# Slots 8 to 31 as pairs of 64-row matmuls that trade banks midway, in an attention and bilinear feed-forward kernel on one core

## The chip, the core and the metric

One of the eight cores of a Trainium2 chip runs the kernel. TensorE (PE) multiplies, with a weight load (PEld) ahead of each matmul; ScalarE (ACT) does exp and copies, VectorE (DVE) multiplies and copies, GpSimd (POOL) and SyncE (SP) issue DMAs. The metric is the device time of one execution in microseconds (us); less is better. PSUM, into which TensorE writes, has eight banks of 512 fp32 columns in 128 partitions; SBUF holds everything else.

## The reference

```python
# q, k, v: (8, 8, 576, 64); bias_table: (32, 8); all fp32
scores = (1 / sqrt(64)) * q @ k.T                  # 576 x 576 for each batch and head
scores = scores + bias_table[bucket(|i - j|)]      # 32 buckets, the last from distance 128 on
attn = exp(scores - max); attn = attn / attn.sum(-1)
x = (attn @ v) as (8 * 576, 8 * 64)                # 4608 tokens, 512 wide
out = ((x @ w_a) * (x @ w_b)) @ w_out              # 512 -> 1536 -> 512
```

## The kernel before

**Attention.** A *slot* s handles one pair p of heads of one batch; there are 32 (eight batches of four). The two heads lie in SBUF partitions 0 to 63 and 64 to 127, so their score matmuls (64 rows of contraction each) are a *pair of 64-row matmuls*: one on the lower, one on the upper half of the array, into different PSUM banks. 576 positions are 512 "main" ones (four tiles of 128) and 64 "tail" ones. All exponentials are taken without a maximum; the bias enters as a factor exp(bias), multiplied on by DVE. The values carry a column of ones, so that the sum of the weights comes out as column 65 (`J = Dh + 1 = 65`).

**Feed-forward.** Tokens are handled in nine chunks of 512 (chunk c is batch c's main positions, the last one all the tails). A chunk has 12 blocks `df`: `pa` and `pb` (each four full matmuls, 128 rows, 512 columns, over `xn_sb`), then ACT copies pa (`ha`), DVE multiplies pb by it (`g_sb[df]`); then four outputs `po` of 12 matmuls each, which ACT copies to SBUF and stores by DMA. That is 144 full matmuls a chunk.

**Order.** It is written by hand: one string of tokens per slot, `steady[s % 4]`, and every engine executes its own instructions in that order. A prime (') means the pair of the slot before. In slots 8 to 31:

- Q0 to Q3 (`qk`, L412): the main scores of one key tile for both heads, into one score tile of two banks; E (`ex`, L440) its exp on ACT, M (`mul`, L446) the factor on DVE.
- R (`qk_rows`, L423): main keys by tail queries, four pairs; ER, MR exp and factor. K (`qk_tail`, L488): tail keys by all queries, 128-row matmuls, where `ZB` has zeros beside each head; EK, MK exp and factor.
- TL' (`av_tails`, L589): tail weights by values, five pairs of 64 rows by 65 columns into two banks, one for each head. A' (`av_head`, L599): main weights by values, 20 matmuls of 128 rows by 65 columns for head 0, then 20 for head 1; a number behind A or F says how many stand there. N0', N1' (`norm_head`, L611): reciprocal and scaling to `XG`, head by head, and then `t_x` (L638), which transposes XG into `xn_sb` by two DMAs on SP.
- F: the next matmul of the feed-forward's stream (`ff_part`, L936), H (`ff_ha`), G (`ff_g`), O and D (`ff_ob`, `ff_store`). F are strewn between the A's.
- MR', V and the loads: V copies values into place; q, k and v of later batches come by DMA from POOL and are transposed by DMA on SP (`t_half`, L388) into `QB`, `KB` and `ZB`.

Slots 0 to 7 and the first chunk stand in another string, `opening`; behind slot 31 the last pair's products (`av`, `av_mm`, its transposes on TensorE) stand between the remaining feed-forward units (`put_units`).

**PSUM.** Pool `ps_sc` has two score tiles of two banks, `ps_ff` two banks for the feed-forward, `ps_av` and `ps_tr` one bank each: the two of `two_banks`, used in turn by R, by TL and A, and by transposes.

Of the kernel before, what the change touches and what calls it, by code (L numbers as in the profile page):

```python
# [13 lines left out]
def kernel(  # L14
# [19 lines left out]
    NM = 4  # L34
# [374 lines left out]
    def shared(p):  # L409
        return p >= 8  # L410

    def qk(p, t0, ts=None):  # L412
        qT, kT, _ = operands(p)
        st[p].setdefault("at", [None] * NM)
        for t in ts or (t0, t0 + 1):
            ps = ps_sc.tile([128, 2, 512], FP32, tag="sc", name=f"qk{p}_{t}")
            for hh in range(2):
                r = slice(64 * hh, 64 * hh + 64)
                nc.tensor.matmul(out=ps[:, hh, :], lhsT=kT[r, t, :], rhs=qT[r, :, :],  # L419
                                 start=True, stop=True)  # L420
            st[p]["ps", t] = ps
# [66 lines left out]
    def qk_tail(p):  # L488
        qT, kT, z = operands(p)
        ps = ps_sc.tile([128, 2, 512], FP32, tag="sc", name=f"qkt{p}")  # L490
        if shared(p):
            nc.tensor.matmul(out=ps[:, 0, :], lhsT=z[:, 1, :], rhs=qT[:, :, :], start=True, stop=True)  # L492
            nc.tensor.matmul(out=ps[:, 1, 0:2 * ST], lhsT=z[:, 1, :], rhs=z[:, 0, :],
                             start=True, stop=True)
            st[p]["ps"] = (ps, None)
            return
# [15 lines left out]
    def ex_tail(p):  # L512
# [5 lines left out]
        if shared(p):  # L518
            nc.scalar.activation(out=at[:, 512:m + 2 * ST],
                                 in_=ps[:, :, :].rearrange("p a x -> p (a x)")[:, 0:SM + 2 * ST],  # L520
                                 func=ACTF.Exp, scale=scale)
            return
# [7 lines left out]
    def mul_tail(p):  # L530
        if not shared(p):
            mul_rows(p)
        at, wt = st[p]["att"], Wt_sb[:, p % 4, :]
        o = 512 + main_tail(p) - 128
        nc.vector.tensor_tensor(out=at[:, o:o + 256], in0=at[:, o:o + 256], in1=wt[:, 255::-1], op=MULT)
# [51 lines left out]
    J = Dh + 1  # L587

    def av_tails(p):  # L589
        b, hp = divmod(p, 4)  # L590
        st[p]["av2"] = banks = two_banks(f"av{p}")
        for jq in range(5):
            for hh in range(2):
                r = slice(64 * hh, 64 * hh + 64)
                nc.tensor.matmul(out=banks[hh][:, J * jq:J * jq + J], lhsT=weights_tail(p, jq)[r, :],  # L595
                                 rhs=vt[b % 2][r, hh, hp, :], start=(jq == 0), stop=True,
                                 skip_group_check=True)

    def av_head(p, hh):  # L599
        b, hp = divmod(p, 4)  # L600
        bank, v = st[p]["av2"][hh], vm[b % 2]

        def mm(jq, t):
            w = weights_last(p, t) if jq == 4 else weights(p, t, hh, jq)
            return lambda: nc.tensor.matmul(out=bank[:, J * jq:J * jq + J], lhsT=w,  # L605
                                            rhs=v[:, 2 * hp + hh, t, :], start=False, stop=True,
                                            skip_group_check=True)

        return [mm(jq, t) for jq in range(5) for t in range(NM)]

# [162 lines left out]
    def v_next(s):  # L773
# [135 lines left out]
    for token in opening.split():  # L909
# [26 lines left out]
    def ff_part(n):  # L936
        c, u, m = 1 + (n // 4 - 48) // 36, (n // 4 - 48) % 36, n % 4
        if u < 24:
            df, (w, kind) = u // 2, ((wa_sb, "pa"), (wb_sb, "pb"))[u % 2]
            if m == 0:  # L940
                ff[kind, df, 0] = ff_bank(f"{kind}{c}_{df}")
            nc.tensor.matmul(out=ff[kind, df, 0][:, :], lhsT=w[df // 4][:, m, 128 * (df % 4):128 * (df % 4) + 128],  # L942
                             rhs=xn_sb[m][:, 512 * c:512 * c + 512], start=(m == 0), stop=(m == NMC - 1))
        else:
            tt, part = divmod(u - 24, 3)
            if part == 0 and m == 0:
                ff["po", tt] = ff_bank(f"po{c}_{tt}")
            df = 4 * part + m
            nc.tensor.matmul(out=ff["po", tt][:, :], lhsT=g_sb[df][:, 128 * tt:128 * tt + 128],  # L949
                             rhs=wo_sb[:, df, :], start=(df == 0), stop=(df == NDF - 1))  # L950
        if m == 3 and (u < 24 or u % 3 == 2):
            ff["done"][u] = c

    ff["done"] = {}
    ff["mm"] = 4 * nxt
    ff["skip"] = 108 - sum(int(x[1:]) for k in (1, 2, 3) for x in steady[k].split() if x[0] == "F")

    def slot_step(s, token):
        name, num = token.rstrip("'0123456789"), "".join(x for x in token if x.isdigit())
        if name in ("F", "A"):  # L960
            for _ in range(int(num)):
                if name == "F" and ff["skip"] > 0:
                    ff["skip"] -= 1
                elif name == "F":
                    ff_part(ff["mm"])
                    ff["mm"] += 1
                elif av_queue:
# [54 lines left out]
    load_slot = {bb: 9 if bb == 3 else 12 if bb == 4 else 4 * bb - 5 for bb in range(3, B)}  # L1022
    while ff["skip"] < 0:
        ff_part(ff["mm"])
        ff["mm"] += 1
        ff["skip"] += 1
    for s in range(8, NP):
# [11 lines left out]
        for token in steady[s % 4].split():  # L1039
            slot_step(s, token)  # L1040
    for token in steady[0].split():
        if token.endswith("'") and token[0] in "EM":
            slot_step(NP, token)
    while ff["mm"] % 4:
        slot_step(NP, "F1")
    for u in sorted(ff["done"]):
        for name in (("O", "D") if u >= 24 else ("G",) if u % 2 else ("H",)):
            slot_step(NP, f"{name}{u}")
    nxt = ff["mm"] // 4
    ff["late"] = True  # L1050
    trb[0] = ps_tr.tile([128, 1024], BF16, tag="tr", name="trz")
    p = NP - 1
    av(p, (0, 1, 2))
    put_units(3)
    av(p, (3, 4))
    t_x(p, (0, 1, 2))
    put_units(3)
    t_x(p, (3, 4))
    put_units(len(units) - nxt)
# [30 lines left out]
```

## Time and profile before

| | |
|---|---|
| time, median of 3 runs | 410.97 us (410.04 to 411.16) |
| profiled execution | 411.31 us, of it the span of the core 409.5 us |
| granted TensorE clock | 0.999 of full speed |
| TensorE busy | 396.5 us, 97% of the span |
| slots 8 to 31 | from 71 to 332 us of the span |
| feed-forward after that | to about 405 us |

Lines of the profile read: start or count, busy time in us, engine, the line of the kernel (L419), operation, output tile <- input tiles, shape, and in brackets or behind a bar the idle time before it and what ended it. "64\*128 64x512" is a matmul on 64 rows and 128 columns of the array with 512 columns streamed. Busy times of matmuls overlap: they are pipelined.

### The profile page before, as it was taken

The numbers are of one execution on the slowest core, as the hardware profiler recorded it, in microseconds if no ns is written. First come the engines' busy times: TensorE is split into PE (matmuls) and PEld (weight loads), VectorE is DVE, ScalarE is ACT, GpSimd is POOL, SyncE is SP. The second block draws the span as 40 slices with busy tenths as digits, with TensorE's granted clock in tenths as the row PEclk, the third lists the DMA queues.
The fourth block names the chain that finished last, engine by engine and source line by source line (L and its number), as shares of the span: only waits on it lengthen the run. The fifth ranks groups of instructions, "written<-read, shape, count | busy, mean of one in ns | idle before, by whom it ended". The sixth has DMA issues, their size and how long they took to land.

```text
span 409.5 us, 9141 instructions
## 1 busy us (share of the span) xinstructions
PE 396.5 (97%) x3618; PEld 208.0 (51%) x3678; DVE 242.3 (59%) x568; ACT 252.2 (62%) x386; POOL 131.5 (32%) x188
## 2 busy tenths in 40 slices
PE   6999999999999999999999999999999999999995
PEld 2576656455555555455554455555555554444443
DVE  4799997357746675577657774577466752321420
ACT  4998993566756776775767666667567742323321
POOL 5976465878069003920095007000000000000000
PEclk9999999999999999999999999999999999999999
DMA  9999999999899827990399729640620012002004
GB/s 150 178 213 197 206 139 139 161 210 144 89 132 181 126 17 102 187 160 18 68 143 153 104 40 143 102 90 17 109 64 17 14 42 77 2 26 78 1 11 94
DMA packets 135964, 42.40 MB, mean 104 GB/s; under 512 B 113544, under 2 KB 131176, under 8 KB 135920
## 3 DMA queue, kind: packets, MB, share of 16 engines
q0 software_dynamic: 81120, 19.88, 53.8%
q1 hardware_dynamic: 49456, 12.61, 20.2%
q10 hardware_dynamic: 5344, 9.31, 6.9%
q8 instruction: 29, 0.48, 0.5%
q14 instruction: 15, 0.12, 0.1%
HBM read 39.23 MB, written 9.45 MB: 119 GB/s over the span
## 4 chain that ended last, share of the span: by engine, by line
PE 95%; DMA 1%; issue 1%; ACT 1%; DVE 0%; SPq 0%; ACTq 0%
PE po L949 15%; PE pa L942 15%; PE pb L942 15%; PE av L605 9%; PE pa L680 8%; PE pb L680 8%; PE qk L419 7%; PE po L717 7%; PE av L582 2%; PE qkt L492 1%; DMA xn<-in_k_dram 1%; PE qkh L459 1%; PE av L595 1%; PE av L572 1%; PE qr L429 1%
## 5 line engine op out<-in xcount | busy, mean ns | idle before, releaser
L443 ACT ACTIVATE at<-qk 128x1024 bf16<-128x1024 f32 x112 | 112.2, 1023 | 26.9 <-PE qk L419 26.3
L690 DVE TENSOR_TENSOR g<-pb,ha 128x512 bf16<-128x512 f32 (+1 forms) x114 | 75.5, 662 | 68.2 <-PE pb L680 40.0
L687 ACT ACTIVATE ha<-pa 128x512 f32<-128x512 f32 (+1 forms) x114 | 65.9, 578 | 68.6 <-PE pa L680 29.7
L448 DVE TENSOR_TENSOR at<-at,W 128x1024 bf16<-128x1024 bf16 x112 | 76.0, 686 | 10.4 <-ACT at L443 9.3
L942 PE MATMUL pa<-xn,wa 128*128 128x512 bf16 x262 | 80.4, 379 | 0.7
L942 PE MATMUL pb<-xn,wb 128*128 128x512 bf16 x278 | 77.8, 379 | 0.0
L949 PE MATMUL po<-wo,g 128*128 128x512 bf16 x277 | 69.7, 379 | 0.8 <-issue 0.8
L605 PE MATMUL av<-vm,at 128*128 128x65 bf16 x736 | 69.0, 194 | 0.6
L605 PEld LDWEIGHTS <-at 128*128 128x128 bf16 x736 | 46.9, 98 | 23.4 <-issue 1.4
L726 ACT ACTIVATE ob<-po 128x512 f32<-128x512 f32 x34 | 20.5, 604 | 48.7 <-PE po L949 21.5
L614 DVE RECIPROCAL rh<-av 128x5 f32<-128x5 f32 x46 | 8.9, 194 | 53.4 <-PE av L605 53.4
L136 POOL DMA_DIRECT2D qn<-in_q_dram x48 | 36.2, 800 | 10.2 <-PE trb L505 8.3
L949 PEld LDWEIGHTS <-g 128*128 128x128 bf16 x288 | 27.0, 98 | 23.4 <-issue 0.4
L942 PEld LDWEIGHTS <-wb 128*128 128x128 bf16 x288 | 27.0, 98 | 22.7
L680 PE MATMUL pa<-xn,wa 128*128 128x512 bf16 (+1 forms) x165 | 37.8, 349 | 0.2
L680 PE MATMUL pb<-xn,wb 128*128 128x512 bf16 (+1 forms) x164 | 37.7, 348 | 0.2
L174 POOL DMA_DIRECT2D vt<-in_v_dram x12 | 7.5, 643 | 94.0 <-PE av L595 89.1
L145 POOL DMA_DIRECT2D kn<-in_k_dram x48 | 36.2, 783 | 2.4 <-DMA qn<-in_q_dram 1.5
L942 PEld LDWEIGHTS <-wa 128*128 128x128 bf16 x288 | 26.2, 98 | 16.5
L419 PE MATMUL qk<-QB,KB 64*128 64x512 bf16 x192 | 30.0, 381 | 0.0
L717 PE MATMUL po<-wo,g 128*128 128x512 bf16 x128 | 29.2, 379 | 0.2
L605 PE MATMUL av<-vm,att 128*128 128x65 bf16 x184 | 24.2, 194 | 0.7
(120 smaller groups left out, 442.3 us busy)
## 6 DMA issues: line engine op xcount, KB each, us to landing
out_dram<-ob ACTq DMA_DIRECT2D x31, 256.0 KB, 2.8
vn<-in_v_dram POOLq DMA_DIRECT2D x16, 256.0 KB, 5.4
kn<-in_k_dram POOLq DMA_DIRECT2D x48, 64.0 KB, 4.9
qn<-in_q_dram POOLq DMA_DIRECT2D x48, 64.0 KB, 5.2
wa<-in_moe_w_a_dram POOLq DMA_DIRECT2D x3, 512.0 KB, 8.3
wb<-in_moe_w_b_dram POOLq DMA_DIRECT2D x3, 512.0 KB, 8.3
wo<-in_moe_w_out_dram POOLq DMA_DIRECT2D x1, 1536.0 KB, 15.9
xn<-XG SPq DMA_TRANSPOSE x52, 3.7
```

Source lines behind the costliest of these rows:

```text
L136: nc.gpsimd.dma_start(out=by_tile(qn[b % 2])[:, h0 // 4, t, :, :], in_=q[b, h0:h1, 128 * t:128 * t + 128, :].transpose([1, 0, 2]))
L145: nc.gpsimd.dma_start(out=by_tile(kn[b % 2])[:, h0 // 4, t, :, :], in_=k[b, h0:h1, t:SM:NM, :].transpose([1, 0, 2]))
L419: nc.tensor.matmul(out=ps[:, hh, :], lhsT=kT[r, t, :], rhs=qT[r, :, :], start=True, stop=True)
L443: nc.scalar.activation(out=at[:, :, :], in_=ps[:, :, :], func=ACTF.Exp, scale=scale)
L448: nc.vector.tensor_tensor(out=at[:, :, :], in0=at[:, :, :], in1=w[:, :, S - 1 + t:S - 1 + t - SM:-1], op=MULT)
L605: return lambda: nc.tensor.matmul(out=bank[:, J * jq:J * jq + J], lhsT=w, rhs=v[:, 2 * hp + hh, t, :], start=False, stop=True, skip_group_ ...
L680: nc.tensor.matmul(out=ps[:, 0:n], lhsT=w[df // 4][:, mc, 128 * (df % 4):128 * (df % 4) + 128], rhs=xn_sb[mc][:, 512 * c + lo:512 * c + lo ...
L687: nc.scalar.activation(out=ha[:, 0:n], in_=ff["pa", df, lo][:, 0:n], func=ACTF.Copy)
L690: nc.vector.tensor_tensor(out=g_sb[df][:, lo:lo + n], in0=ff["pb", df, lo][:, 0:n], in1=ff["ha", df, lo][:, 0:n], op=MULT)
L717: nc.tensor.matmul(out=po[:, :], lhsT=g_sb[df][:, 128 * tt:128 * tt + 128], rhs=wo_sb[:, df, :], start=(df == 0), stop=(df == NDF - 1))
L942: nc.tensor.matmul(out=ff[kind, df, 0][:, :], lhsT=w[df // 4][:, m, 128 * (df % 4):128 * (df % 4) + 128], rhs=xn_sb[m][:, 512 * c:512 * c ...
L949: nc.tensor.matmul(out=ff["po", tt][:, :], lhsT=g_sb[df][:, 128 * tt:128 * tt + 128], rhs=wo_sb[:, df, :], start=(df == 0), stop=(df == ND ...
```

## The change

1. *Pairs everywhere in slots 8 to 31.* `row_pair` issues two 64-row matmuls, one on each half of the array, into two banks. A full 128-row matmul becomes two halves. Two accumulations that go together (pa and pb of a block; two po; the two heads of A; the two halves of the K scores) run side by side: first the lower rows of one with the upper rows of the other, over the whole accumulation, and then, after a *swap*, the other two halves, so that each bank gets both halves of its sum and no bank is written from both halves at once. At the swap stands `keepalive_nop`, an instruction of TensorE's sequencer that names the two output banks as inputs. One F is now such a pair (144 a chunk, as before), and one A too (40 a slot, as before).
2. *K* is now K (one half, and the tail by tail part) and KB (the other half), with a swap between them. The score tile's layout for it changes, and with it the operands of EK, MK and `weights_tail`.
3. *PSUM:* all of Q, K and KB share one score tile, `steady_sc[0]`; the second `ps_sc` tile becomes two more feed-forward banks, so that pairs of banks alternate.
4. *Order:* the four strings are new. Both heads of A end together, so N0' and N1' stand behind all 40 A. H and G of a block can only start when pa and pb are both done. F counts per slot (s % 4 = 0, 1, 2, 3) are 48, 34, 31, 31 in place of 38, 36, 35, 35.
5. *Ends:* the opening's last four units (FO00 to FO02, HO0: the first po) move to slot 8, which begins with Q0. Behind slot 31 the last pair's TL', A, N follow in the new form with 24 F pairs between, and its transposes go by DMA on SP like the others'.

```diff
+    def qk_keys(p, part):
+        qT, _, z = operands(p)
+        if part == 0:
+            st[p]["ps"] = (score_tile(p), None)
+        ps = st[p]["ps"][0]
+        halves = (ps[:, 0, 0:256], qT[:, 2:4, :]), (ps[:, 1, ST:256 + ST], qT[:, 0:2, :])
+        row_pair(*((halves[hh ^ part][0], z[:, 1, :], halves[hh ^ part][1], part == 0, True) for hh in range(2)),
+                 key="keys", turn="swap" if part else None)
+        if part == 0:
+            row_pair(*((ps[:, hh, 256 - 256 * hh:256 - 256 * hh + ST], z[:, 1, :],
+                        z[:, 0, ST * hh:ST * hh + ST], False, True) for hh in range(2)), key="keys", turn="last")
+    def score_tile(p):
+        return steady_sc[0] if p >= 8 else ps_sc.tile([128, 2, 512], FP32, tag="sc", name=f"qk{p}")
...
+    def row_pair(lo, hi, key=None, turn=None):
+        if turn == "swap":
+            nc.tensor.keepalive_nop([nc.tensor.lower_ap(lo[0]), nc.tensor.lower_ap(hi[0])])
+        for r, (o, lhs, rhs, first, last) in ((LO, lo), (HI, hi)):
+            i = nc.tensor.matmul(out=o, lhsT=lhs[r], rhs=rhs[r], start=first, stop=last, skip_group_check=True)
...
-    def av_head(p, hh):
+    def av_pairs(p):
...
+        def operands_of(hh, jq, t):
             w = weights_last(p, t) if jq == 4 else weights(p, t, hh, jq)
+            return banks[hh][:, J * jq:J * jq + J], w, v[:, 2 * hp + hh, t, :], False, True
+        return [lambda x=x, jq=jq, t=t: row_pair(operands_of(x, jq, t), operands_of(1 - x, jq, t),
+                                                 "av", {(0, 4, 3): "last", (1, 0, 0): "swap"}.get((x, jq, t)))
+                for x in range(2) for jq in range(5) for t in range(NM)]
...
-        if 4 <= p < NP - 1:
+        if p >= 4:
...
     steady = {
         1: """
+            Q0 F4 TL' A8 F2 A2 F2 E0 A2 F1 A2 F1 A1 F1 H0 A1 F1 M0 Q1 A4 F1 E1 G1 F1 A2 F1 A1 F1 A1
+            F1 H2 M1 Q2 F1 A1 E2 A1 F1 G3 A1 F1 A13 F1 N0' Q3 F1 E3 F2 N1' F3 H4 F1 M3 R K ER F1 G5
+            KB F1 EK F1 M2 F2 H6 F1 MK
         """,
         2: """
+            Q0 F1 G7 E0 F1 TL' A8 MR' A1 F2 V F1 A1 Q1 F1 E1 F2 A10 F1 H8 F1 A5 Q2 A1 G9 A1 F1 E2
+            A3 F2 M1 A2 F2 H10 M2 F3 G11 Q3 A8 E3 F1 N0' F4 N1' H12 F1 K F2 G13 KB R EK F1 M3 F2 ER
+            F1 MK F1 M0
         """,
         3: """
+            Q0 H14 F2 E0 F1 G15 TL' A9 MR' A2 F2 A2 Q1 A4 F1 E1 F1 A1 F1 A2 F2 H16 A1 F1 A4 Q2 G17
+            A2 F1 E2 A5 F1 M0 F1 A1 F2 M2 H18 F3 G19 Q3 A7 F1 E3 N0' F4 N1' H20 F1 K F2 G21 KB R EK
+            F3 ER F1 MK
         """,
         0: """
+            Q0 M3' F1 E0 F2 M1' F2 V TL' H22 F1 MR' F1 A1 Q1 G23 F1 E1 A5 F1 A3 F2 A3 F1 A8 Q2 F1
+            E2 F2 A1 F3 A1 F1 A1 F1 A6 F1 A4 F1 A1 F1 A2 F1 A2 F1 A2 Q3 N0' F1 E3 F3 N1' F2 O26 F2
+            M3 F1 D26 K F1 M1 F1 KB R M0 F1 ER F2 O29 F1 MR F2 D29 F2 EK F3 MK F1 M2 O32 D32 O35
+            D35
         """,
...
+    steady_sc.append(ps_sc.tile([128, 2, 512], FP32, tag="sc", name="score"))
+    pair = ps_sc.tile([128, 2, 512], FP32, tag="sc", name="ffn_pair")
+    steady_ff.append([pair[:, i, :] for i in range(2)])
+    steady_ff.append([ps_ff.tile([128, 512], FP32, tag="ffn", name=f"ffn{i}")[:, :] for i in range(2)])
+    def ff_part():
+        c, f = ff["chunk"], ff["mm"]
+        if f < 96:
+            n, (x, i) = f // 8, divmod(f % 8, 4)
+            banks = steady_ff[n % 2]
+            units = [(banks[y], w[n // 4][:, i, 128 * (n % 4):128 * (n % 4) + 128],
+                      xn_sb[i][:, 512 * c:512 * c + 512], f % 8 == 0, f % 8 == 7) for y, w in enumerate((wa_sb, wb_sb))]
         else:
+            n, (x, i) = (f - 96) // 24, divmod((f - 96) % 24, 12)
+            banks = steady_ff[n % 2]
+            units = [(banks[y], g_sb[i][:, 128 * tt:128 * tt + 128], wo_sb[:, i, :],
+                      (f - 96) % 24 == 0, (f - 96) % 24 == 23) for y, tt in enumerate((2 * n, 2 * n + 1))]
+        m = 3 if f < 96 else 11
+        row_pair(units[x], units[1 - x], "ffn", {(0, m): "last", (1, 0): "swap"}.get((x, i)))
...
+    last = [x for x in steady[0].split() if x.endswith("'") and x[0] in "EM"]
+    last += [x for x in steady[0].split() if x[0] in "HG"]
+    for token in last + "TL' A20".split():
+        slot_step(NP, token)
+    while ff["mm"] != 108:
+        ff_part()
+    slot_step(NP, "A20")
+    for token in ("N0'", "N1'"):
+        slot_step(NP, token)
+    while ff["mm"] != 120:
+        ff_part()
```

More of the change, by code (lines that the diff above doesn't have):

```diff
@@ L309 @@
     st = [dict() for _ in range(NP)]
+    steady_sc, steady_ff = [], []
     trb = [ps_tr.tile([128, 1024], BF16, tag="tr", name="trb")]
@@ L415, in qk @@
         for t in ts or (t0, t0 + 1):
[L416 to L420, printed above, removed]
+            ps = score_tile(p)
+            row_pair(*((ps[:, hh, :], kT[:, t, :], qT[:, :, :], True, True) for hh in range(2)))
             st[p]["ps", t] = ps
@@ L490, in qk_tail @@
         ps = ps_sc.tile([128, 2, 512], FP32, tag="sc", name=f"qkt{p}")
[L491 to L496, printed above, removed]
         for t in range(NM):
@@ L518, in ex_tail @@
         if shared(p):
-            nc.scalar.activation(out=at[:, 512:m + 2 * ST],
-                                 in_=ps[:, :, :].rearrange("p a x -> p (a x)")[:, 0:SM + 2 * ST],
-                                 func=ACTF.Exp, scale=scale)
+            nc.scalar.activation(out=at[:, 512:m + 2 * ST].rearrange("p (a x) -> p a x", a=2),
+                                 in_=ps[:, :, 0:256 + ST], func=ACTF.Exp, scale=scale)
             return
@@ L533, in mul_tail @@
         at, wt = st[p]["att"], Wt_sb[:, p % 4, :]
-        o = 512 + main_tail(p) - 128
+        o = 512 + (128 if shared(p) else main_tail(p) - 128)
         nc.vector.tensor_tensor(out=at[:, o:o + 256], in0=at[:, o:o + 256], in1=wt[:, 255::-1], op=MULT)
@@ L554, in weights_tail @@
     def weights_tail(p, jq):
+        if shared(p):
+            o = 512 + (384 + 128 * jq if jq < 2 else 256 if jq == 4 else 128 * jq - 256)
+            return st[p]["att"][:, o:o + 128]
         if jq == 4:
@@ L587 @@
     J = Dh + 1
+    LO, HI = slice(0, 64), slice(64, 128)
+    def row_pair(lo, hi, key=None, turn=None):
[3 more added lines that the diff above has]
+            i = nc.tensor.matmul(out=o, lhsT=lhs[r], rhs=rhs[r], start=first, stop=last, skip_group_check=True)
     def av_tails(p):
@@ L592, in av_tails @@
         for jq in range(5):
[L593 to L597, printed above, removed]
-    def av_head(p, hh):
+            row_pair(*((banks[hh][:, J * jq:J * jq + J], weights_tail(p, jq), vt[b % 2][:, hh, hp, :], jq == 0, True)
+                       for hh in range(2)))
+    def av_pairs(p):
         b, hp = divmod(p, 4)
-        bank, v = st[p]["av2"][hh], vm[b % 2]
-        def mm(jq, t):
+        banks, v = st[p]["av2"], vm[b % 2]
+        def operands_of(hh, jq, t):
             w = weights_last(p, t) if jq == 4 else weights(p, t, hh, jq)
[L605 to L609, printed above, removed]
+            return banks[hh][:, J * jq:J * jq + J], w, v[:, 2 * hp + hh, t, :], False, True
+        return [lambda x=x, jq=jq, t=t: row_pair(operands_of(x, jq, t), operands_of(1 - x, jq, t),
+                                                 "av", {(0, 4, 3): "last", (1, 0, 0): "swap"}.get((x, jq, t)))
+                for x in range(2) for jq in range(5) for t in range(NM)]
     def norm_head(p, hh):
@@ L800 @@
         M60 S63 E63 FA8f HA8f T7 ET7 M63 M70 FB8f G8f AV60 FA9f FB9f N60 MT7 AV70 HA9f G9f FA10f HA10f
-        FB10f N70 AV71 G10f FA11f HA11f FB11f N71 X71 AV61 X70 FO00 G11f N61 FO01 FO02 CX71:D CX70:D HO0
+        FB10f N70 AV71 G10f FA11f HA11f FB11f N71 X71 AV61 X70 G11f N61 CX71:D CX70:D
     """
@@ L914 @@
         1: """
-            Q0 TL' Q1 A5 F1 A2 E0 A7 F1 A2 F1 A1 F1 A1 F1 H0 A2 F1 N0' A2 F1 E1 A2 F1 A3 F1 G1 A1
-            F1 A1 F1 A1 F1 M1 A7 H2 A2 F1 A1 F1 N1' F3 Q2 G3 Q3 E2 R M0 F4 H4 F3 E3 K G5 F3 M2 F2
-            H6 F1 M3 F2 EK F2 ER F1 MK F1 G7
+            Q0 F4 TL' A8 F2 A2 F2 E0 A2 F1 A2 F1 A1 F1 H0 A1 F1 M0 Q1 A4 F1 E1 G1 F1 A2 F1 A1 F1 A1
+            F1 H2 M1 Q2 F1 A1 E2 A1 F1 G3 A1 F1 A13 F1 N0' Q3 F1 E3 F2 N1' F3 H4 F1 M3 R K ER F1 G5
+            KB F1 EK F1 M2 F2 H6 F1 MK
@@ L918 @@
         """,
         2: """
-            Q0 H8 Q1 MR' TL' E1 A5 F1 A2 F1 A1 F1 E0 A1 F1 A4 F1 G9 A4 F1 A2 F1 M1 A2 F1 A3 F1 H10
-            N0' A1 F1 A1 F1 A2 F1 A1 F1 A1 G11 A2 F1 A3 F1 A3 F1 A2 F1 H12 N1' F3 Q2 V Q3 G13 E2 R
-            F4 M2 F1 H14 F3 E3 K G15 F3 EK M0 F2 ER F1 MK F1 M3 H16
+            Q0 F1 G7 E0 F1 TL' A8 MR' A1 F2 V F1 A1 Q1 F1 E1 F2 A10 F1 H8 F1 A5 Q2 A1 G9 A1 F1 E2
+            A3 F2 M1 A2 F2 H10 M2 F3 G11 Q3 A8 E3 F1 N0' F4 N1' H12 F1 K F2 G13 KB R EK F1 M3 F2 ER
+            F1 MK F1 M0
@@ L923 @@
         """,
         3: """
-            Q0 Q1 MR' TL' A2 F1 A1 F1 A1 G17 A8 F1 A2 F1 A2 F1 A1 F1 H18 A3 F1 N0' A1 F1 E0 A2 F1
-            A2 F1 G19 A4 F1 E1 A4 F1 A5 F1 A2 F1 H20 N1' F3 Q2 G21 Q3 E2 R F1 M0 F3 M2 F1 H22 F2 K
-            E3 F3 G23 F1 EK F2 M1 ER F2 MK F1 M3 F2
+            Q0 H14 F2 E0 F1 G15 TL' A9 MR' A2 F2 A2 Q1 A4 F1 E1 F1 A1 F1 A2 F2 H16 A1 F1 A4 Q2 G17
+            A2 F1 E2 A5 F1 M0 F1 A1 F2 M2 H18 F3 G19 Q3 A7 F1 E3 N0' F4 N1' H20 F1 K F2 G21 KB R EK
+            F3 ER F1 MK
@@ L928 @@
         """,
         0: """
-            Q0 MR' Q1 TL' A3 F1 A2 F1 A1 F1 O26 A1 F1 A4 F1 E1 A2 F1 A2 F1 A2 F1 D26 A1 F1 A2 E0 F1
-            N0' A3 F1 A3 F1 A6 F1 A2 F1 A2 F1 O29 A2 F1 A1 F1 A1 D29 F1 N1' F3 Q2 M1 Q3 E2 R F4 ER
-            M2 F2 E3 K MR F1 V F2 M0 EK F3 O32 MK F1 M3 F2 D32 F2 O35 D35
-        """,
-    }
[L936 to L943, printed above, removed]
-        else:
[L945 to L952, printed above, removed]
@@ new lines @@
+    steady_ff.append([ps_ff.tile([128, 512], FP32, tag="ffn", name=f"ffn{i}")[:, :] for i in range(2)])
[6 more added lines that the diff above has]
+                      xn_sb[i][:, 512 * c:512 * c + 512], f % 8 == 0, f % 8 == 7) for y, w in enumerate((wa_sb, wb_sb))]
+        else:
+            n, (x, i) = (f - 96) // 24, divmod((f - 96) % 24, 12)
[4 more added lines that the diff above has]
+        row_pair(units[x], units[1 - x], "ffn", {(0, m): "last", (1, 0): "swap"}.get((x, i)))
+        if f < 96 and f % 8 == 7:
+            ff["pa", n, 0], ff["pb", n, 0] = banks
+            ff["done"].update({2 * n: c, 2 * n + 1: c})
+        elif f >= 96 and (f - 96) % 24 == 23:
+            ff["po", 2 * n], ff["po", 2 * n + 1] = banks
+            ff["done"].update({26 + 6 * n: c, 29 + 6 * n: c})
+        ff["mm"] = (f + 1) % 144
+        ff["chunk"] += ff["mm"] == 0
@@ L954 @@
     ff["done"] = {}
-    ff["mm"] = 4 * nxt
-    ff["skip"] = 108 - sum(int(x[1:]) for k in (1, 2, 3) for x in steady[k].split() if x[0] == "F")
+    ff["chunk"], ff["mm"] = 0, 96
     def slot_step(s, token):
@@ L961, in slot_step @@
             for _ in range(int(num)):
[L962 to L966, printed above, removed]
+                if name == "F":
+                    ff_part()
                 elif av_queue:
@@ L994, in slot_step @@
             av_tails(p)
-            av_queue[:] = av_head(p, 0) + av_head(p, 1)
+            av_queue[:] = av_pairs(p)
         elif name == "R":
@@ L998, in slot_step @@
         elif name == "K":
-            qk_tail(p)
+            qk_keys(p, 0)
+        elif name == "KB":
+            qk_keys(p, 1)
         elif name == "E":
@@ L1022 @@
     load_slot = {bb: 9 if bb == 3 else 12 if bb == 4 else 4 * bb - 5 for bb in range(3, B)}
[L1023 to L1026, printed above, removed]
+    for _ in range(96 - ff["mm"]):
+        ff_part()
     for s in range(8, NP):
@@ L1040 @@
             slot_step(s, token)
[L1041 to L1049, printed above, removed]
-    ff["late"] = True
[L1051 to L1058, printed above, removed]
+    last = [x for x in steady[0].split() if x.endswith("'") and x[0] in "EM"]
[3 more added lines that the diff above has]
+    while ff["mm"] != 108:
+        ff_part()
+    slot_step(NP, "A20")
+    for token in ("N0'", "N1'"):
+        slot_step(NP, token)
+    while ff["mm"] != 120:
+        ff_part()
+    for u in (26, 29):
+        slot_step(NP, f"O{u}")
+        slot_step(NP, f"D{u}")
+    ff["late"] = True
+    nxt = 48 + 36 * (NCH - 4) + 30
     put_units(len(units) - nxt)
```

## The prediction

> **What bounds the kernel now.** I read the page's head and its chain of waits first.
>
> ```profile
> span 409.5 us, 9141 instructions
> PE 396.5 (97%) x3618; PEld 208.0 (51%) x3678; DVE 242.3 (59%) x568; ACT 252.2 (62%) x386; POOL 131.5 (32%) x188
> PE 95%; DMA 1%; issue 1%; ACT 1%; DVE 0%; SPq 0%; ACTq 0%
> ```
>
> TensorE is busy from end to end and is 95% of the chain; ACT and DVE have a third of their time free. So a change is worth what it takes off TensorE's own steps, less the waits that it opens. Busy time cannot show such steps (a 512-column matmul is drawn 0.379 us long, but the next starts 0.216 us after it), so I went on to the timeline of TensorE and measured from start to start.
>
> ```profile
> 199.98 2.32 PE L949 MATMUL po<-wo,g 128*128 128x512 bf16 x10
> 202.23 0.61 PE L419 MATMUL qk<-QB,KB 64*128 64x512 bf16 x4
> 202.68 0.32 PE L595 MATMUL av<-vt,att 64*128 64x65 bf16 x10
> 202.93 0.24 PE L605 MATMUL av<-vm,at 128*128 128x65 bf16 x2
> ```
>
> Ten full matmuls of 0.216 end their turn at 202.14, yet the 64-row score matmuls begin at 202.23: 0.09 us is lost where the array goes from 128 to 64 rows. Four of them (two pairs) take 0.45, so a pair costs 0.216 like one full matmul, plus about 0.01 after the change. The ten 64x65 matmuls take 0.25: five pairs of 0.030 and again 0.095 on the way back. The same timeline gives the length of a period of four slots, from the start of slot 13 to that of slot 17, and the price of the tail pairs with no change of rows behind them:
>
> ```profile
> 126.72 0.39 PE L419 MATMUL qk<-QB,KB 64*128 64x512 bf16 x2
> 126.94 0.31 PE L595 MATMUL av<-vt,att 64*128 64x65 bf16 x10
> 127.09 0.38 PE L419 MATMUL qk<-QB,KB 64*128 64x512 bf16 x2
> ...
> 170.12 0.39 PE L419 MATMUL qk<-QB,KB 64*128 64x512 bf16 x2
> ```
>
> Period 43.40 us; a 65-column pair 0.150/5 = 0.030. The sum of the steps of a period: F 144 x 0.216 = 31.10, A 160 x 0.031 = 4.96 (nine from 127.79 to 128.07), TL 20 x 0.030 = 0.60, Q 16 x 0.216 = 3.46, R 16 x 0.029 = 0.46, K 4 x (0.216 + 0.056) = 1.09; together 41.67. What is left, 1.73, is the 16 changes of row mode, 0.108 each: in these slots TensorE waits for nobody.
>
> **What the change takes away.** Sums go against the profiled execution, 411.31 us (span 409.5 and 1.8 around it); the median of the runs is 0.34 lower.
> - Changes of row mode: 4 in each of 24 slots, 96 x 0.108 = 10.4. F, A and K become 64-row pairs, so none is left there; two stand at the ends (0.2).
> - K: 0.272 becomes two 256-column pairs and a 64-column pair, 0.109 + 0.109 + 0.029 = 0.247; 24 x 0.025 = 0.6.
> - A: 0.031 becomes a 65-column pair, 0.030 by L595, or 0.0325 by the longest run of single ones (27 in 0.92 us, three of them of 0.06). I take 0.0305, nearer the pair: 920 x 0.0005 = 0.5; ends +0.9 and -1.4.
> - F: 0.216 either way by L419; the count is the same. Score, row and tail pairs were pairs before.
> - Pair 31: its old products and transposes take 0.95 + 0.78 + 0.11 = 1.84 (332.77 to 333.72, 336.31 to 337.09, 339.68 to 339.79); the new ones 5 x 0.030 + 40 x 0.0305 = 1.37: 0.5.
>
> Gain 12.0.
>
> **What it adds.** *Swaps.* Each accumulation now changes halves midway, and the nop ahead of the second half names both banks, so TensorE's sequencer stands there until the last pair of the first half has ended, with everything behind it queued. No row shows this wait. Nearest rows: a 512-column matmul ends 0.380 after its start; TensorE starts 0.05 after what it waits for (below: 7.43 to 7.48); its waiting sequencer instructions are drawn 0.051 long. So 0.484 from the last pair's start, 0.27 beyond its own 0.216. A wait costs only what the work queued between lacks of 0.27:
>
> ```profile
> 7.00 0.43 DVE L326 CAST kn<-xn 128x512 bf16<-128x512 f32 x1 [1.94 <-DMA xn<-in_k_dram]
> ...
> 7.48 0.64 PE L334 MATMUL trk<-cn_sb,kn 128*64 128x128 bf16 x8 [1.37 <-DVE kn L326]
> ```
>
> From the new order, a period has 22 swaps, with between the halves (us): slot 0 0.46, 0.23, A 0.86, K 0.43; slot 1 0.39, 0.34, 0.39, 0.26, A 0.43, K 0.22; slot 2 0.42, 0.43, 0.46, 0.23, A 0.43, K 0.43; slot 3 0.48, 0.40, 0.43, 0.23, A 0.43, K 0.43. Short are five, by about 0.04 each (0.01 at 0.26): 0.18 a period, 1.1 in six. Ends: 0, and 132 x 0.27 = 36 if nothing covers them.
>
> *One score tile.* A score pair must wait for the exp before it: 0.38 + 0.04 + 1.02 (L443) + 0.05 = 1.49 from pair to pair. The new order leaves 1.54 and 1.57 where it is tightest (slot 1, Q1 to Q2 to Q3), and 1.09 against 1.08 from KB over the 0.71 exp of the keys to the next slot's Q0. ACT is free then. I take 0.1 a period, 0.6; ends 0 and 2. In slot 8, which has no A yet, Q1 to Q2 has 1.30: 0.2.
>
> *Slot 8's first scores.* Twelve po matmuls (71.19 to 73.87) leave the opening for slot 8, behind Q0. Q0 reads QB, whose transpose is issued at 63.52:
>
> ```profile
> 63.52 2.37 SPq L391 DMA_TRANSPOSE QB<-qn  x1
> ```
> ```profile
> DMA to landing us min/median/max: 7.3/8.4/9.5
> ```
>
> It lands at 73.02. The old order needed it at 73.87; the new one is there at 71.19 and waits 1.9, with all of slot 8 queued behind. What is late next, the tail keys in ZB (75.96), is needed ten us later. Ends 0.5 and 2.5.
>
> *The norms.* Both heads now end together, so N0' and N1' come after all of A: the last XG is written 0.18 + 0.73 + 0.23 + 0.43 = 1.57 after the last A (rows L614, L615, L618), and the fourth F of slots 13, 17, 21, 25, 29 reads its transpose. From that write to this F there is 4.83 of TensorE work. These transposes land after 5.3, 5.1, 5.8, 5.5 and 2.5 (those issued at 121.9, 165.3, 208.7, 252.1, 295.5; over all "2.4/3.9/5.9" to landing), and 0.1 is lost around them: short by 0.5, 0.4, 1.1, 0.8, 0. Loads run beside them as before, but the write comes some 2 us later against their start. I take 2.2 of the 2.8; ends 0 and 4. R waits for the norms too, with 0.16 to spare.
>
> *Four feed-forward banks.* Pa and pb end together; ha (0.60) and g (0.69) have eight F (1.73) until the bank returns: nothing.
>
> *The end.* After slot 31 nothing stands between MK and TL'. From the start of KB: keys ready 0.28, exp to 1.03, MK to 1.36; TensorE has R and four F, until 1.09, and waits 0.3. M3', M1' and MR' follow on DVE (0.61 a step), M1' ends at 2.57, and the second A needs it: 1.1 more. 1.4 in all. The transposes of pair 31 now go by DMA, 2.5 to 5.5, under 36 F (7.8): nothing.
>
> Costs: 0.2 + 1.1 + 0.6 + 0.2 + 1.9 + 2.2 + 1.4 = 7.6. Net -4.4: 411.31 - 4.4 = 406.9, and 406.6 against the median.
>
> [...] A stream of A pairs means four instructions in 0.030 us. The trace: ten matmuls of L595 in 0.150, 0.015 each; and here sixteen run at 0.014 each straight after a wait of the array:
>
> ```profile
> 22.21 0.44 PE L343 MATMUL trb<-cn_sb,qn 64*64 64x64 bf16 x16 [0.19 <-ACT xn L324]
> ```
>
> [...]
>
> **Rivals.**
> 1. *Every wait is hidden*: swaps, score tile and norms cost 0 to 1.8 instead of 3.9; 406.6 - 3.9 = 402.7, to 404.5. For it: before, no wait shows, and the covers look cut to size. Against: the landing times.
> 2. *The gain is eaten*: norms at 4, score tile at 2, A at 0.0325: 411.31 - 10.1 + 10.8 = 412.0, or 411.7 against the median. This is the case of no change, 409.7 to 412.2.
> 3. *Slower by the swap*: if the sequencer's restart costs more than my 0.1. At a need of 0.42 beyond the pair instead of 0.27 the shorts sum to 1.12 a period instead of 0.18, 5.6 us more: the gain of 4.4 is gone from about 0.39. At 0.63 they are 5.3 a period, 31 us more: 437. For it: it is the one wait that no row shows, 132 times. Against: 0.05 restarts.
> 4. *Slower by the feed*: instructions on TensorE per slot grow from about 200 to 350. Its densest 6 us hold 255 weight loads and matmuls (23.5 ns each, from 18.1); the new A stretches want 240 in 4.4 us (18 ns). [...] It decides from 0.18 a slot. Against: row L343.
> 5. *The pairs do not run together*: F would cost 0.43, 187 us more. L419 speaks against it in every slot.
>
> **Chances.** My sum, 404.5 to 409.7: 0.48, likeliest near 406.6. Rival 1: 0.16. Rival 2: 0.12. Rival 3: 0.11. Rival 4: 0.10. Rival 5 and mishaps of that size: 0.03. About 0.3% (1.2 us) is what a measurement can tell from no change: faster 0.64, same 0.12, slower 0.24. The range 402.7 to 414.0 leaves out a little of rival 1 and most of rivals 3 to 5, some 0.2.
>
> **What would show it.** Right: in slots 8 to 31 no 128-row matmul and no steps of 0.311; a period near 42.2; F starts 0.216 apart, A pairs 0.030; TensorE's first wait at 71.2 for QB near 1.9; its waits at the fourth F of slots 13, 17, 21, 25 between 0.3 and 1.1; 1.4 behind slot 31. Wrong: waits of 0.2 or more at most swaps (rival 3), A pairs over 0.036 (rival 4), or waits of TensorE for ACT at the score pairs in every slot (rival 2).

## The result, and the profile after

The changed kernel takes 423.72 us (median of 4 runs, 422.27 to 426.04) against 410.74 us before: ratio 1.032, 95% interval 1.027 to 1.037. It is slower by 13 us; forecast was faster by 4.4. The profiled execution took 426.04 us, the one before 411.31, so the two traces differ by 14.7.

First the head of the page, its chain of waits, and the instruction queue with its packets, MB and share of the DMA engines:

```profile
span 424.3 us, 13133 instructions
PE 398.5 (94%) x5614; PEld 234.6 (55%) x5626; DVE 241.3 (57%) x565; ACT 257.2 (61%) x386; POOL 131.6 (31%) x188
q8 instruction: 44, 0.72, 0.7%
PE 76%; DMA 15%; ACT 4%; DVE 1%; issue 1%; POOL 1%; ACTq 1%; SPq 0%; POOLq 0%; DVEq 0%
```

TensorE was 95% of the chain; now DMA holds 15% and ACT 4%. Then the matmul side, in the timeline of TensorE:

```profile
160.76 0.28 PE L604 MATMUL av<-vm,at 64*128 64x65 bf16 x6
160.85 0.31 PE L604 MATMUL av<-vm,att 64*128 64x65 bf16 x8
160.98 0.37 PE L604 MATMUL ffn_pair<-xn,wb 64*128 64x512 bf16 x1
161.00 0.37 PE L604 MATMUL ffn_pair<-xn,wa 64*128 64x512 bf16 x1
161.20 0.38 PE L604 MATMUL ffn_pair<-xn,wb 64*128 64x512 bf16 x1
```

Seven A pairs in 0.22 us (0.031 each), the two halves of an F 0.02 apart and the next F 0.22 later, and nothing lost where A, F and scores meet. The pairs do what they promise. What is new stands in the list of TensorE's waits (us in all, times, longest); none of its first three rows had a counterpart in the kernel before:

```profile
PE ffn_pair L604 <- DMA xn<-XG: 7.8, 4, 3.7
PE ffn L604 <- ACT ob L740: 3.4, 3, 1.9
PE score L604 <- DMA QB<-qn: 2.4, 1, 2.4
PE av L604 <- issue: 1.2, 1, 1.2
```

Measured from the last start before a wait, less that instruction's own step, they come to 8.5, 3.8, 2.6 and 1.4. The first, in the timeline of TensorE, and the clock after it, by windows (length, then busy us of PE, PEld, DVE, ACT and POOL with the count of instructions, the granted clock, DMA share, GB/s):

```profile
130.28 0.38 PE L604 MATMUL ffn_pair<-xn,wa 64*128 64x512 bf16 x1
130.30 0.38 PE L604 MATMUL ffn_pair<-xn,wb 64*128 64x512 bf16 x1
134.39 0.58 PE L604 MATMUL ffn_pair<-xn,wa 64*128 64x512 bf16 x1 [3.71 <-DMA xn<-XG]
```
```profile
130.28:134.20 3.92, 0.40 (x4) 0.09 (x1) 0.09 (x1) 0.53 (x1) 1.28 (x3) 1.00 1.65 169
134.20:137.60 3.40, 3.21 (x46) 1.92 (x47) 0.00 (x0) 1.02 (x3) 1.57 (x3) 0.50 1.97 194
137.60:143.37 5.77, 5.77 (x105) 3.35 (x100) 4.33 (x11) 5.00 (x7) 2.34 (x4) 1.00 1.12 143
```

This is the fourth F of slot 13. The transpose that it reads was issued at 125.58 and landed 8.8 us later; then 3.4 us ran at half clock. Where the transpose stands against the loads is in the timelines of POOL (the first row of the burst) and SP, of the kernel before and then of the changed one:

```profile
116.49 1.23 POOL L174 DMA_DIRECT2D vt<-in_v_dram  x2 [13.07 <-PE av L595]
121.94 1.21 SPq L642 DMA_TRANSPOSE xn<-XG  x1
```
```profile
118.45 1.22 POOL L174 DMA_DIRECT2D vt<-in_v_dram  x2 [11.07 <-PE av L604]
125.58 1.54 SPq L656 DMA_TRANSPOSE xn<-XG  x1
```

It is issued 7.13 us into the burst instead of 5.45. The step from slot 12's to slot 13's R took 16.54 us (126.83 to 143.37). In e8 (below), where nothing disturbs it, it took 11.13:

```profile
123.79 0.30 PE L443 MATMUL qr<-ZB,KB 64*128 64x64 bf16 x8
134.92 0.29 PE L443 MATMUL qr<-ZB,KB 64*128 64x64 bf16 x8
```

The difference is 3.89 of wait and 1.5 of slow clock. The second kind, in the timeline of ACT:

```profile
224.46 0.60 ACT L740 ACTIVATE ob<-ffn 128x512 f32<-128x512 f32 x1 [1.85 <-DMA out_dram<-ob]
225.09 0.34 ACTq L747 DMA_DIRECT2D out_dram<-ob  x1
228.32 0.60 ACT L740 ACTIVATE ob<-ffn 128x512 f32<-128x512 f32 x1 [3.26 <-DMA out_dram<-ob]
228.94 0.34 ACTq L747 DMA_DIRECT2D out_dram<-ob  x1
229.33 1.02 ACT L456 ACTIVATE at<-score 128x1024 bf16<-128x1024 f32 x1 [0.41 <-ACT ob L740]
```

O26 to O35 of a chunk now stand close together at the end of the slots divisible by four, and share two SBUF buffers. The last copy waits for an earlier store to land, the `ffn` bank stays full, and E0 of the next slot (229.33) is queued behind it on ACT: TensorE waits 2.1 for the bank, 0.5 for E0, and again a stretch of half clock follows (229.8).

By periods, from one R to the R four slots on: 47.49, 45.67, 47.56 and 45.06 for those that start at slots 12, 16, 20 and 24, and 42.55 for the one from slot 25 to 29, in which no loads are left to run. Before, every one was 43.40.

### The profile page after: what moved, and what is told of

Read it like the earlier page. It is cut to its first block, busy times and chain, and to the rows that moved or that the text cites. A ratio compares the mean times of both kernels' runs of the same rounds, so it can differ in the third digit from the quotient of the medians.

```text
span 424.3 us, 13133 instructions
## 1 busy us (share of the span) xinstructions
PE 398.5 (94%) x5614; PEld 234.6 (55%) x5626; DVE 241.3 (57%) x565; ACT 257.2 (61%) x386; POOL 131.6 (31%) x188
## 4 chain that ended last, share of the span: by engine, by line
PE 76%; DMA 15%; ACT 4%; DVE 1%; issue 1%; POOL 1%; ACTq 1%; SPq 0%; POOLq 0%; DVEq 0%
PE ffn_pair L604 22%; PE ffn L604 19%; PE av L604 8%; PE score L604 6%; PE po L731 5%; PE pb L694 5%; PE pa L694 5%; DMA out_dram<-ob 4%; DMA wo<-in_moe_w_out_dram 4%; DMA QB<-qn 2%; DMA xn<-XG 2%; PE qkh L472 1%; ACT ob L740 1%; DMA xn<-in_k_dram 1%; DMA vn<-in_v_dram 1%
## 5 line engine op out<-in xcount | busy, mean ns | idle before, releaser
L456 ACT ACTIVATE at<-score 128x1024 bf16<-128x1024 f32 x96 | 98.4, 1025 | 53.8 <-PE score L604 50.0
L604 PE MATMUL ffn_pair<-xn,wa 64*128 64x512 bf16 x288 | 82.2, 380 | 7.8 <-DMA xn<-XG 7.8
L604 PE MATMUL ffn<-xn,wb 64*128 64x512 bf16 x288 | 82.2, 380 | 3.4 <-ACT ob L740 3.4
L604 PE MATMUL ffn<-xn,wa 64*128 64x512 bf16 x288 | 82.5, 380 | 0.0
L604 PE MATMUL ffn_pair<-xn,wb 64*128 64x512 bf16 x288 | 82.3, 381 | 0.0
L604 PEld LDWEIGHTS <-at 64*128 64x128 bf16 x1536 | 53.7, 95 | 30.9 <-issue 9.0
L604 PE MATMUL av<-vm,at 64*128 64x65 bf16 x1536 | 68.6, 192 | 0.6 <-DVE at L461 0.6
L604 PEld LDWEIGHTS <-wb 64*128 64x128 bf16 x576 | 47.6, 95 | 19.9 <-issue 10.2
L604 PEld LDWEIGHTS <-wa 64*128 64x128 bf16 x576 | 47.4, 95 | 18.4 <-issue 0.4
L704 DVE TENSOR_TENSOR g<-pb,ha 128x512 bf16<-128x512 f32 (+1 forms) x42 | 25.8, 614 | 45.6 <-PE pb L694 45.1
```

Source lines behind the costliest of these rows:

```text
L456: nc.scalar.activation(out=at[:, :, :], in_=ps[:, :, :], func=ACTF.Exp, scale=scale)
L604: i = nc.tensor.matmul(out=o, lhsT=lhs[r], rhs=rhs[r], start=first, stop=last, skip_group_check=True)
L704: nc.vector.tensor_tensor(out=g_sb[df][:, lo:lo + n], in0=ff["pb", df, lo][:, 0:n], in1=ff["ha", df, lo][:, 0:n], op=MULT)
```

## The experiments

**The loads.** One burst of loads sits where the waits are: POOL's queue waits for TL' of a batch's last slot (`load_vt`), and then sends some 17 us of k, q and v loads (116.49 to 133.57 in the kernel before), into the norms, transposes and stores that end the batch. *e1* starts the burst about two slots later, *e7* does the same to the kernel before, *e6* leaves it out, *e10* leaves it in place but thinner.

```diff
-                if s == load_slot[bb] + (2 - (bb < 5)) * g:
-                    load_half(bb, g)
+        if s in (9, 10, 11):
+            for bb, g in {9: [(3, 0)], 10: [(3, 1), (4, 0)], 11: [(4, 1)]}[s]:
+                load_half(bb, g)
+        elif s % 4 == 3 and s // 4 + 2 < B:
+            load_v(bb, 4, 8)            # bb = s // 4 + 2; waits for V of slot s - 1
+            load_half(bb, 0)
+            load_k(bb, 4, 8)
+            load_q(bb, 4, 8)
```

> Only the order of the loads for the batches 4 to 7 is changed, so that POOL's main burst of loads starts about two slots later and no longer beside the transposes that end a batch and the output stores. Theory 1 (these transposes and stores land late because they share the DMA engines with the burst): the four waits of TensorE for xn, 8.5 us in the changed kernel, fall below 1 in all, the waits for ACT's output copies (3.8) fall too, and the time is 410 to 414. Theory 2 (the transposes are late because both norms now come after all of A, and the order of SP's queue makes it worse; the loads are innocent): the xn waits stay above 6 and the time is 420 to 425. Under both the wait of slot 8 for QB stays at 2 to 2.6.

408.64 us, ratio to the kernel before 0.9966 (0.9941 to 0.9991): below either range. All xn waits are gone, and so are all waits for output copies, with two buffers as before. Theory 1.

> The kernel before with the later loads of e1 and nothing else: the control. Theory 1 (in the kernel before every late landing was covered): 409.5 to 411, no change. Theory 2 (the early burst cost the kernel before too, so that e1's gain is no gain of the change): 405 to 408.

411.34 us, ratio 1.0006 (0.9993 to 1.0018), and every period is 43.40 again. The burst cost the kernel before nothing; its place matters only to the new order.

*e6* is the changed kernel with `if bb < 4 and s == load_slot[bb] + ...`; it leaves out the loads of batches 4 to 7, whose slots then compute on old data:

> The changed kernel as it is, with the k, q and v loads of batches 4 to 7 left out (their slots compute on old data); order, buffers and instruction streams of TensorE, ACT and DVE are untouched. Theory 1 (all three kinds of stall, xn, output buffers, instruction fetch, come from transfers that share the DMA engines with these loads): their sum, 15 us, falls below 1.5; QB's 1.7 to 2.6 and the end's 1.25 stay; the time is 406 to 409. Theory 2 (two output buffers are too few in any case, and the norms too late in any case): the waits for output copies stay above 3 or the xn waits above 3, and the time is 411 to 417.

407.57 us. No xn wait, no wait for a copy, no wait without a semaphore; QB's wait 1.27, the end 1.25. In its trace the stores land after a median of 2.0 us instead of 3.8. Waits of 0.46 at a Q1 remain at three places, 1.4 in all: ACT's last copy of a chunk still waits for an earlier store (1.30 at 86.00, 1.20 at 212.91), with E0 behind it. But for these, two buffers and late norms are enough when nothing else is in flight.

*e10* adds to `load_k` and `load_q`, after each 64 KB load:

```diff
+            if b >= 4:
+                for _ in range(2):
+                    nc.gpsimd.memset(zero_sb[:, :], 0.0)
```

> The changed kernel with its loads in their old place and order, but POOL clears a scratch tile twice after each 64 KB k or q load of batches 4 to 7 (an estimate of 0.5 to 1 us), so that fewer loads are queued at a time. Theory 1 (what is late is late because a backlog of queued loads stands ahead of it on the DMA engines): with the backlog gone the waits for xn and for output copies halve or better, 409 to 416. Theory 2 (any load running at the same time delays them): the loads now run for longer, the waits stay, 419 to 425.

408.75 us, ratio 0.9952 (0.9930 to 0.9975). POOL's timeline, of the changed kernel and then of e10, shows the pace:

```profile
118.45 1.22 POOL L174 DMA_DIRECT2D vt<-in_v_dram  x2 [11.07 <-PE av L604]
119.65 2.99 POOL L145 DMA_DIRECT2D kn<-in_k_dram  x4
```
```profile
119.06 0.78 POOL L151 DMA_DIRECT2D kn<-in_k_dram  x1
119.80 1.15 POOL L144 MEMSET zero_sb<- 128x512 bf16 x2
120.90 0.75 POOL L151 DMA_DIRECT2D kn<-in_k_dram  x1
121.64 0.55 POOL L144 MEMSET zero_sb<- 128x512 bf16 x1
```

And the DMA issues (KB each, median us to landing), in the same order:

```profile
kn<-in_k_dram POOLq DMA_DIRECT2D x48, 64.0 KB, 6.5
out_dram<-ob ACTq DMA_DIRECT2D x31, 256.0 KB, 3.8
```
```profile
kn<-in_k_dram POOLq DMA_DIRECT2D x48, 64.0 KB, 4.1
out_dram<-ob ACTq DMA_DIRECT2D x31, 256.0 KB, 2.5
```

The same loads from the same point, one in 1.85 us instead of 0.75 (the two memsets take 1.15), and 15 us come back; one xn wait of 1.5 is left, no wait for a copy. So here it was the backlog of queued loads that made the others late, not a load as such.

**The output buffers.** *e2*: `ob` gets a buffer of its own for each tile of a chunk.

```diff
-        ob = ob_last if (c, tt) == (0, 2) else wrk.tile([128, DM], FP32, tag="ob", ...)
+        if tt < 2:
+            ob = wrk.tile([128, DM], FP32, tag="ob", ...)
+        else:
+            ob = ob_last if tt == 2 and c < B else ob_fourth     # tlc[0], free after the opening
```

> Only the output copies get four SBUF buffers, one for each tile of a chunk, in place of two. Theory 1 (ACT stands behind the landing of an earlier store because two buffers serve four copies that now come close together): TensorE's waits for ACT's copies, 3.8 us, and the waits at the Q1 behind them, 1.4, go; the xn waits stay near 8.5; the time is 417 to 420. Theory 2 (freeing ACT only lets TensorE run into the next late landing): the xn waits grow by as much, and the time stays at 422 to 425.

412.66 us, ratio 1.0048 (1.0027 to 1.0069): lower than both theories said. The copies' waits and those at the Q1 behind them are gone, as theory 1 has it. But the xn waits shrank too, 8.5 to 5.9, against theory 2 and against "stay near 8.5" of theory 1, and no stretch of half clock followed a wait in the steady slots. Why the transposes land earlier with more output buffers is not settled. The two remedies overlap: e1 and e2 each take away most of the loss.

**What is left when the waits are repaired.** *e3* joins e1 and e2, and moves F at both ends:

```diff
-    for _ in range(96 - ff["mm"]):
+    for _ in range(12):                 # slot 8 skips every fourth F in return
         ff_part()
...
+    for _ in range(6):                  # after slot 31, ahead of TL'
+        ff_part()
```

> The changed kernel with the later loads, the four output buffers, twelve pairs of the first chunk's last products put back in front of slot 8, and six pairs put in front of the tail products behind slot 31. If waits are the whole of the loss: QB's wait of 2.6 and the end's 1.25 go too, periods are near 42.5 us, and the time is 405 to 409, faster than the kernel before by 2 to 6 us. If the pairs themselves or the granted clock cost time, it stays at 411 or above, with no wait of TensorE to show for it.

407.67 us, ratio 0.9949 (0.9924 to 0.9974): faster than the kernel before, by 0.5%. QB's wait and the end's are gone, but the profile shows four stalls of TensorE that no semaphore ends. Three are those that the expectation of e5 names, 0.84, 2.39 and 0.39 us; the fourth is 1.00, at a score pair that was due at 247.67. The longest and the fourth:

```profile
192.28 0.37 PE L605 MATMUL ffn<-xn,wb 64*128 64x512 bf16 x1
192.30 0.37 PE L605 MATMUL ffn<-xn,wa 64*128 64x512 bf16 x1
194.89 0.37 PE L605 MATMUL ffn<-xn,wb 64*128 64x512 bf16 x1 [2.22 <-issue]
248.67 0.39 PE L605 MATMUL score<-QB,KB 64*128 64x512 bf16 x2 [0.82 <-issue]
```

In the trace the instruction queue (q8) moves 16 KB at a time; one such transfer starts at 191.7, in the burst of loads, takes 1.3 us, and TensorE goes on 1.9 us after its end (1.3 to 1.9 at the stalls of the changed kernel, e1, e2, e3, e5, e9 and e11). The pairs raised the program from 9141 to 13133 instructions and this queue from 29 to 44 transfers. *e8* is e3 without the loads of batches 4 to 7 (old data again), *e5* splits the burst in two:

> The kernel of e3 with the k, q and v loads of batches 4 to 7 left out (old data in their slots). Theory 1 (fetches late behind loads): no stall without a semaphore above 0.2 us after slot 11 and no clock drop; 403 to 405.5. Theory 2 (the fetches are too slow for this density of instructions by themselves): stalls stay, 407 to 408.

404.74 us (404.63 to 405.32), ratio 0.9854 (0.9840 to 0.9869). No stall without a semaphore, 17 of 20 periods at 41.96 to 42.10, and the fetch in question starts 1.5 us after its slot's R instead of 4.8 (e5), while the transfer itself takes 1.3 and 1.4. Theory 1, with one thing more exact: behind the loads the fetch begins late; it does not run longer.

> The kernel of e3 with each batch's loads split into two bursts (half of the k and q loads go behind the vt loads, one slot group later) and eight in place of twelve pairs ahead of slot 8. Theory 1 (the stalls of TensorE without a semaphore, 0.84, 2.39 and 0.39 us in e3 and 1.38 in the changed kernel, are its own instruction fetches that land late behind a long burst of loads): they fall below 1.5 in all and no clock drop follows; the time is 404.5 to 407. Theory 2 (they come from the count of instructions alone, whatever the loads do): they stay at 2.5 or more, 407 to 409. The part of the loads that now starts at the tail products of a batch's last slot may bring up to 2 us of xn waits back.

```diff
-            load_k(bb, 4, 8)
-            load_q(bb, 4, 8)
+        if s % 4 == 1 and 5 <= b < B:
+            load_k(b, 4, 8)
+            load_q(b, 4, 8)
```

407.14 us, ratio 0.9912 (0.9891 to 0.9934), a hair above the range: 0.84, 0.39 and 1.00 are gone, 2.39 became 1.84 and no half clock follows. It probably stays because the first burst, issued from 180.66 to 193.55, still reaches that fetch (191.6). *e11* asked whether this is chance (it is the kernel of e9, below, once more, and has no pauses in spite of its label):

> The kernel of e9 once more, one look for its profile: whether the stall of 1.8 us without a semaphore at 192 us in e5 is the same in every execution. If a fetch is late by its place against the burst, it is there again within 1 us of the same size and time; if by chance, it is gone or elsewhere.

The one execution took 409.55 us. In e5, e9 and e11 the stall is 1.84, 1.84 and 1.84, at the same F; the one near 107 us is 1.63 in e9 and 0.56 in e11. The first is a matter of place, the other varies.

**Whole rows in the new order.** *e4* is e3 with one 128-row matmul in place of each F and A pair:

```diff
-        row_pair(units[x], units[1 - x], "ffn", {(0, m): "last", (1, 0): "swap"}.get((x, i)))
+        o, lhs, rhs, first, last = units[x]
+        nc.tensor.matmul(out=o, lhsT=lhs, rhs=rhs, start=(i == 0), stop=(i == m - 1), ...)
```

> The kernel of e3 in the same order, but the feed-forward and attention-value matmuls use all 128 rows again (one matmul for each pair, no swap of banks). The order then has 56 changes of row mode in four slots, none in e3. Theory 1 (a change of row mode costs 0.108 us, pairs cost what whole matmuls cost): 6 x 56 x 0.108 = 36 us more than e3, 441 to 446. Theory 2 (the saving per change is smaller where short stretches follow each other, or pairs cost more than whole matmuls): 5 to 25 us more than e3.

435.37 us, ratio 1.0608 (1.0583 to 1.0633): 27.7 above e3, between the theories. Its timeline, with a change of row mode ahead of the scores and one behind them:

```profile
149.67 1.03 PE L977 MATMUL ffn_pair<-xn,wa 128*128 128x512 bf16 x4
150.62 0.39 PE L605 MATMUL score<-QB,KB 64*128 64x512 bf16 x2
150.95 0.30 PE L623 MATMUL av<-vm,at 128*128 128x65 bf16 x4
```

From the second row to the third 0.33 pass for a pair of 0.216: 0.11. A period is 47.58 with 56 changes and 42.09 without (e8): 5.49, or 0.098 a change. That is net of the swaps: e8's period holds 0.46 of waits at swaps of F (below), which e4 does not have. With them the change alone is 5.95 / 56 = 0.106, as the row says and theory 1 has it. The totals stand nearer because e4 has no fetch stall (29 transfers again), while the profiled e3 loses 4.6 to its four and 1.5 to a stretch of half clock.

**The swap.** Slot 8 of e5 has two swaps with nothing between the halves, and shows a wait of 0.33 at each. *e9* moves twelve pairs ahead of slot 8 and skips F in its second half, so that a score pair stands between:

> The kernel of e5 with twelve pairs ahead of slot 8 again, but the twelve F that slot 8 then gives up are taken from its second half, so that the swaps of its two last-product units each have a score pair between their halves. In e5 slot 8 shows two swap waits of 0.33 us and waits of 0.29, 0.21 and 0.64 before score pairs. If a swap's wait is only the rest of its 0.55 us that no other work covers, both swap waits go, and with them 0.5 to 1.2 us of slot 8: 405.9 to 407. If the swap costs by itself, they stay and the time is 407 or more.

Of 0.33 each, 0.10 and 0.11 are left: 0.33 less the 0.22 of the score pair between. So a swap cost here what was uncovered. The time is 407.93, ratio 0.9934 (0.9909 to 0.9959), above the range: with nine F skipped behind KB, slot 9's Q0 waits 1.9 for the exp of the tail keys, which stands on ACT behind ER and the output copy O29.

Last, *e12* is e9 with the pauses of e10:

> The kernel of e9 with the pauses of e10 in POOL's loads. Theory 1 of e10: instruction fetches no longer stand behind a backlog either, the stall of 1.8 us goes, 404.5 to 406.5, the fastest of all. Theory 2: the same as e9 or slower.

407.10 us, ratio 0.9893 (0.9865 to 0.9921), above the range of theory 1. No stall without a semaphore, as it says; but spread out, the split loads reach the ends of batches again, and two xn waits of 1.5 and 1.8 take the gain. Of the kernels that compute the whole output, e5 and e12 are the fastest, 3.5 to 3.9 us below the kernel before.

## Why the prediction was wrong

The matmul part held. Without the burst of loads (e6) the profiled execution takes 406.90 us, and 411.31 - 4.4 = 406.9 was the sum. That nearness is partly luck, as the terms show.

- **Changes of row mode**: taken at 0.108, measured 0.106 (e4, with the swaps' waits added back): this term held. An A pair takes 0.0316, not 0.0305.
- **Swaps**: the need beyond the pair was put at 0.27 and is 0.33. At the covers of 0.22, 0.23 and 0.26 TensorE waits 0.07 to 0.11 behind R and KB (e1's last period), 0.46 a period or 2.8 in all instead of 1.1. With that need the covers of the text itself give 0.48. With all of this a clean period gains 43.40 - 42.09 = 1.31; the terms for A, K, row mode, swaps and score tile gave 1.63. Swaps take 0.28 more than that and A 0.18 more; the 0.1 for the score tile does not occur in a clean period.
- **Score tile**: taken 0.8 with slot 8; the waits at Q1 and Q2 of all slots come to 1.9 in the changed kernel, 1.7 in e6, most of it 0.46 at a time at the Q1 behind a chunk's output copies.
- **QB**: taken 1.9, measured 2.57 here and 1.2 to 2.5 where e1, e2, e6 and e10 left slot 8 alone, against ends of 0.5 and 2.5. **The end**: taken 1.4, measured 1.25.
- **The norms: the step that failed.** The text saw the wait, at the right F and on the right slots, and priced it at 2.2 with landing times of the kernel before (5.1 to 5.8), because "Loads run beside them as before". It added that the write comes 2 us later against their start, and gave that no price. Measured, the transposes are issued 7.1 us after the burst begins instead of 5.45, and land after 8.8, 7.0, 6.3 and 6.0: 8.5 us, beyond the upper end of 4. The work that covers a landing was right (4.83 from the write in the text, 4.93 from the issue to the moment the F was due); the landing time was not. e1, e6 and e10 show that the loads make it late. How much of the lateness comes from the 1.7 us of later start, and how much from the stores and fetches that now run beside it, was not separated.
- **"Four feed-forward banks: nothing"** looked at ha and g alone. The po banks go back through ACT's copy, the copy needs an SBUF buffer, the buffer a landed store: 3.8, with E0 queued behind. The row was among the waits of the kernel before, and was not followed; here it is before and after (us in all, times, longest):

```profile
ACT ob L726 <- DMA out_dram<-ob: 6.0, 3, 2.0
```
```profile
ACT ob L740 <- DMA out_dram<-ob: 28.9, 13, 4.2
```

- **Rival 4** had the feed of instructions as a rate, at 23.5 ns each. Twenty A pairs on end at 0.032 each (e8, behind slot 31), 8 ns an instruction, say that the rate is no limit there, and e8 has no stall at all. What was real is the fetch behind it: 1.4 here, and in the repaired kernels with loads 0.9 to 4.6, or nothing where the loads are paced (e10, e12).
- **The clock** had no term: two stretches of 3.4 us at half clock, 1.5 us each.

Together, by the profiled executions: 8.5 + 3.8 + 2.6 + 1.9 + 1.4 + 1.25 + 3.0 = 22.5 lost, 6 x 1.31 + 0.5 = 8.4 won, 14.1 of the 14.7; 0.6 was not traced (the opening, in part at half clock, ends 0.3 later than before). The 12 us of waits for xn and for copies are most of the miss.

## What to carry to other kernels

Price a moved transfer by where it now falls against the other transfers' bursts, not by the landing times of the old order: the same k loads landed after 6.5 us in one burst and after 4.1 when paced, the stores after 3.8 and 2.5. Follow each PSUM bank through its copy and store to the buffer that the copy needs: here a wait of 3.26 us there also held E0, queued behind it on ACT. And pacing a burst of loads by a microsecond of idle work was worth as much here (15 us) as moving it, and more than two more output buffers (11 us).

## What was not expected of the hardware

- The instruction queue makes a transfer of 16 KB for some 250 matmuls and weight loads of TensorE (7296 in 29 transfers before, 11240 in 44 here) while the kernel runs, every 13.6 us before and every 7.5 here (medians). When one began late behind a burst of loads (in e5 4.8 us after its slot's R; in e8, without those loads and without the stall, 1.5), TensorE stalled for 0.25 to 2.4 us, with no semaphore in the profile to show it; stall and transfer are tied by their times alone.
- After waits of 3.89 and of 2.10 with 0.46 (changed kernel), 2.39 (e3) and 2.46 us (e10, at QB) the granted clock was 0.50 for exactly one stretch of 3.4 us; after waits of 2.57 (changed kernel), 2.35 (e2) and 1.93 (e9), and after 2.13, 0.66 and 0.46 close together (changed kernel, 178 to 184), it stayed at 1.00. So the length of the wait alone does not decide it.
- The same half clock stood over 7.9 to 18.1 us in the opening of the changed kernel, e7 and e9, and over 8.5 to 15.3 in e3, and cost little: slot 8's R came 0.5 later in e7 than in the kernel before, and its first score was due 0.8 later in the changed kernel than in e6, which has the same opening at full clock.
